# Last output rows: three column groups transposed and multiplied before the fourth; last scaling on VectorE; a borrowed score bank in unit 8

## The chip, the core and the metric

The kernel runs on one core of one Trainium2 chip. The metric is the time of one execution on the device, in microseconds, as the median of several runs. Five engines work side by side, each with an in-order queue of its own: TensorE (PE, with its weight loads PEld), VectorE (DVE), ScalarE (ACT), GpSimd (POOL) and SyncE (SP). They wait for each other through semaphores. SP and ACT also issue DMA transfers.

## What is computed

One transformer block on 2048 tokens of width 576, in float32. Six modulation rows come from a small vector c. The attention has 32 heads of 18 and goes through four segments of 512 tokens; a memory M, z is carried from segment to segment.

```python
h = _layernorm(x, axis=-1) * (1 + ca) + sa
# per segment s: masked softmax attention, mixed with the memory's answer
a_dot = softmax(q k^T * scale + mask) @ v
a_mem = (phi(q) @ M) / (phi(q) @ z + 1e-6)
o = g * a_mem + (1.0 - g) * a_dot
M, z = M + phi(k)^T v, z + sum(phi(k))
x = x + ga * (o @ wo)
h = _layernorm(x, axis=-1) * (1 + cb) + sb
x = x + gb * ((_silu(h @ w_gate) * (h @ w_up)) @ w_down)
```

Products are kept near float32 by splitting an operand into a rounded high part and a low rest (`oh` and `ol`, `woh` and `wol`) and adding the products of the parts.

## The kernel before

The work goes in three stages. The first projects q, k, v. The second, in which the change lies, goes through 32 units of four heads of one segment (8 units to a segment), from about 248 to 587 us. The third is the FFN, from 605 us to the end, in two halves of 1024 tokens.

**Order.** Everything in the second and third stage is written out by hand in program order (`tc.manual_schedule`), engine by engine; a tile pool hands out buffers in turn, and an instruction waits for the last user of the buffer that it gets. In the second stage a unit u has 11 steps. At each step one score tile of `p2_step` (line 624: a matmul into a PSUM bank, line 627: its exponential by ACT into `Pt`) and one of `p1_step` for unit u + 2 (line 189, reduced by VectorE on line 194 to row maxima `mx`) are issued, and then the events of the table `PAT`: `V` attention times values (`av`, line 644), `m`/`n` the maxima's transpose (`pmt`, `mr`), `c`/`d` the combination of a unit's result (`px`, line 665; lines 673 to 682), `R`/`S`/`T` transposes of finished output rows and their split (`pto`, lines 726, 733, 737), `Z`/`z` the same for columns 512 to 575 of four rows together (`ptr`, lines 709, 715, 716), `M`/`X` the product with `wo` and the addition of the residual (`pw`, line 753; line 758). Things due later, `stage_a` and `stage_b` among them, are put into `sched` by step.

**PSUM.** It has eight banks. In the second stage they are shared out by tags: `s2` (scores for the exponential, 2 banks), `s1` (scores for the maxima, 2), `x` (2, for `px`, `pmt`, `pto`, `ptr`, `pn`, `pt`), `w` (1) and `av` (1). In units 0 to 3 every third score tile takes a bank of tag `x` in place of one of `s2`. For the last output rows a pool of its own, `pst`, opens over the same banks, with four banks of tag `x` and two of tag `w`.

**stage_b** brings the second segment's half of the FFN's input into place in units 25 to 30: for each of six pieces four transposes of a loaded block (`trans4`, line 971, into `pt`), two scalings by columns (`scaled`, line 966, on ACT, from PSUM into `yo` and `yh`), sums and differences on GpSimd (line 1030), and a split and a store (`y_part`).

**Last output rows.** After unit 31 the fourth segment's 512 rows (`ot[3]`, 4 groups of 128) are multiplied by `wo`. The last unit's combination is the last writer of columns 504 to 575: line 681 and line 682, on VectorE here. Then:

```python
        wo_r(3, 0)
        wo_z(3)
        wo_r(3, 1)
        wo_s(3, 0)
        wo_t(3, 0)
        wo_z2(3)
        wo_s(3, 1)
        wo_t(3, 1)
```

`wo_r` makes four transposes of 128 columns, `wo_z` four of the last 64 columns, `wo_s` casts the transposed tile to `oh` on ACT, `wo_t` takes the rest `ol` on VectorE. Then four times two halves of 288 columns follow with 14 multiplies each: `oh` eight times, `ol` four times, the last 64 columns (`orr`) twice. The transposes of groups 2 and 3 stand behind the multiplies of groups 0 and 1. Weights for the FFN are prepared in between. The addition of the residual for the row group before, (2, 3), is done on VectorE (line 758) just behind line 682, and its store is issued from ACT (line 760).

Of the kernel before, what the change touches and what calls it, by code (L numbers as in the profile page):

```python
# [7 lines left out]
F32 = mybir.dt.float32  # L8
F32R = mybir.dt.float32r
BF16 = mybir.dt.bfloat16  # L10
AF = mybir.ActivationFunctionType
ALU = mybir.AluOpType
# [3 lines left out]
P = 128  # L16
# [49 lines left out]
S1B, S2B, XB, WB = 2, 2, 2, 1  # L66
# [7 lines left out]
def block(ctx: ExitStack, tc: tile.TileContext, x, wqk, wv, wo, beta, wgu, wd, c, w_mod, wm01, out):  # L74
    nc = tc.nc
# [30 lines left out]
    ident = cst.tile([P, P], F32, tag="ident", name="ident")  # L106
# [28 lines left out]
    colm = cst.tile([P, 6, 2], F32, tag="colm", name="colm")  # L135
# [11 lines left out]
    xD = [dr.tile([P, 4, D], F32, tag=f"xD{s}", name=f"xD{s}") for s in range(NSEG)]  # L147
# [11 lines left out]
    turn = [0, 0]  # L159
# [93 lines left out]
    with ExitStack() as p1:  # L253
# [6 lines left out]
        ps = pool(p1, "ps1", 2, space=PSUM)  # L260
# [73 lines left out]
        with ExitStack() as p0:  # L334
# [39 lines left out]
            for b in range(3):  # L374
                n = P if b < 2 else 64
# [233 lines left out]
    def p2_step(u, j):  # L609
        if u >= NU:  # L610
            return
        n = L - 128 * j
        per = L // n if n <= 256 else 1
        pt = pp_.tile([P, 4, n], F32, tag=f"P{j}", name="Pt", bufs=1)
        Pt[u, j] = pt
        for h in range(0, 4, per):
            turn[1] += 1
            if u < 4 and turn[1] % 3 == 0:
                bank = ps.tile([P, L], F32, tag="x", name="s2", bufs=XB)
            else:  # L620
                bank = ps.tile([P, L], F32, tag="s2", name="s2", bufs=S2B)
            for g in range(h, h + per, 2):
                w = min(per, 2)
                nc.tensor.matmul(bank[:, n * (g - h):n * (g - h + w)].rearrange("p (a b) -> p a b", a=w),  # L624
                                 lhsT=kst[u % NB][0:110, g // 2, 128 * j:128 * j + 128],
                                 rhs=qst[u % NB][0:110, g:g + w, 128 * j:L], start=True, stop=True)
            nc.scalar.activation(pt[:, h:h + per, :n], bank[:, :n * per].rearrange("p (a b) -> p a b", a=per),  # L627
                                 AF.Exp, scale=SCALE)
            if h + per < 4:
                yield  # L630
        nc.gpsimd.affine_select(out=pt[:, :, :P], in_=pt[:, :, :P], pattern=[[0, 4], [1, P]], compare_op=ALU.is_ge,
                                fill=0.0, base=0, channel_multiplier=-1)
        yield
# [50 lines left out]
    ot, vq = {}, {}  # L684
# [13 lines left out]
    def yh(k, kb):  # L698
        return yh12[:, k - 1, kb] if k else yh0[:, kb]
# [18 lines left out]
    def load_xr(s, i):  # L718
        xr = o3.tile([P, D], F32, tag="xr", name="xr") if s < 3 or i in (0, 3) else xp.tile([P, D], F32, tag="xs", name="xr")
        nc.sync.dma_start(xr, x[s][:, i, :])  # L720
        return xr

    def wo_r(s, i):
        pt = ps.tile([P, 4, P], F32, tag="x", name="pto", bufs=XB if s < 3 else 4)
        for kt in range(4):
            nc.tensor.transpose(pt[:, kt, :], ot[s][:, i, 128 * kt:128 * kt + 128], ident)
        pto[s, i] = pt
        oh = o3.tile([P, 4, P], F32R, tag="oh", name="oh")
        ol = o3.tile([P, 4, P], F32R, tag="ol", name="ol")
        oT[s, i] = (oh, ol, load_xr(s, i) if s < 3 else xr3[i])  # L730

    def wo_s(s, i):
        nc.scalar.copy(oT[s, i][0], pto[s, i])

    def wo_t(s, i):
        oh, ol, _ = oT[s, i]
# [4 lines left out]
    def wo_m(s, i, h, c, wb=WB):  # L741
        oh, ol, _ = oT[s, i]
        sl = slice(288 * h, 288 * h + 288)
        if c == 0:
            wps[0] = ps.tile([P, L], F32, tag="w", name="pw", bufs=wb)
        ops = []
        for k in range(4):
            ops += [(oh[:, k], woh[:, k, sl]), (oh[:, k], wol[:, k, sl]), (ol[:, k], woh[:, k, sl])]
        if s == 3:
            ops = [ops[n] for n in (0, 1, 3, 4, 6, 7, 9, 10, 2, 5, 8, 11)]  # L750
        ops += [(orr[s][:, i], woh[:, 4, sl]), (orr[s][:, i], wol[:, 4, sl])]
        for n in range(14 * c // WC, 14 * (c + 1) // WC):
            nc.tensor.matmul(wps[0][:, :288], lhsT=ops[n][0], rhs=ops[n][1], start=(n == 0), stop=(n == 13))  # L753

    def wo_x(s, i, h):
        xr = oT[s, i][2]
        sl = slice(288 * h, 288 * h + 288)
        nc.vector.tensor_tensor(xr[:, sl], wps[0][:, :288], xr[:, sl], op=ALU.add)
        if h == 1:
            (nc.scalar if (s, i) == (2, 3) else nc.sync).dma_start(xD[s][:, i, :], xr)  # L760

    lnv = {}

# [197 lines left out]
            for j in range(3):  # L961
                nc.sync.dma_start(dst[:, :, 32 * j:32 * j + 32], src)

    def scaled(dst, pt, kh, kb):
        n, c = P if kb < 2 else 96, 3 * kh + kb
        nc.scalar.activation(dst[:n], pt[:n], AF.Identity, scale=colm[:n, c, 0:1], bias=colm[:n, c, 1:2])

    def trans4(xb, n, pts, key):
# [28 lines left out]
    def stage_b():  # L997
        big = flat(sk2.tile([P, 5, L], F32, tag="pq", name="yq"))
        sts = [big[:, L * i:L * i + L].rearrange("p (a b) -> p a b", b=256).bitcast(F32R) for i in range(2)]
        xb = [big[:, L * i:L * i + L].rearrange("p (a b) -> p a b", b=P) for i in (2, 3)]  # L1000
        sub = flat(opl_.tile([P, 4, D], F32, tag="o1", name="yo"))
        h10 = [sub[:, 256 * i:256 * i + 256] for i in range(2)]
        t3 = [sub[:, 256 * i:256 * i + 256] for i in (2, 3)]
        sto = [sub[:, 1024 + L * i:1024 + L * i + L].rearrange("p (a b) -> p a b", b=256).bitcast(F32R) for i in range(2)]
        pts = {}

        def load(i, hv, kb):
            for kh in range(2):
                load_cols(xb[i % 2][:, 2 * kh:2 * kh + 2], 1, 2 * hv, kh, kb)

        for i in range(6):
            hv, kb = divmod(i, 3)
            u = 25 + i
            n = P if kb < 2 else 96
            c = slice(256 * hv, 256 * hv + 256)
            h00, h01, h11 = [yh(k, kb)[:n, c] for k in range(3)]
            a, b = h10[i % 2], t3[i % 2]
            at(11 * (u - 1) + 1, lambda i=i, hv=hv, kb=kb: load(i, hv, kb))
            g = step_of(u)

            def trans(i=i, n=n):
                trans4(xb[i % 2], n, pts, i)

            def sc(i=i, kb=kb, a=a, c=c):
                pt = flat(pts.pop(i))
                scaled(a, pt[:, 0:256], 0, kb)
                scaled(yh(2, kb)[:, c], pt[:, 256:512], 1, kb)

            def sub2(d, x, y_, op=ALU.subtract):
                nc.gpsimd.tensor_tensor(d, x, y_, op=op)  # L1030
            at(g, trans)
            at(g + 1, sc)
            at(g + 2, lambda b=b, h11=h11, a=a, n=n: sub2(b[:n], h11, a[:n]))
            at(g + 3, lambda h00=h00, a=a, n=n: sub2(h00, a[:n], h00))
            y_part(g + 6, 3, kb, h00, lambda i=i: sto[i % 2], hv)
            at(g + 5, lambda h01=h01, h11=h11: sub2(h01, h01, h11))
            at(g + 7, lambda h00=h00, h01=h01: sub2(h01, h01, h00, ALU.add))
            y_part(g + 4, 5, kb, b, lambda i=i: sts[i % 2], hv)
# [89 lines left out]
    def load_y(t, o):  # L1128
        nc.sync.dma_start(f32(y[:, o, 0:4]), yD[t][o][:, 0:4])
        nc.sync.dma_start(f32(y[0:96, o, 4]), yD[t][o][0:96, 4])  # L1130
# [231 lines left out]
    with tc.manual_schedule():  # L1362
# [40 lines left out]
        load_y(0, 0)  # L1403
        load_o(0, 0, 1)
        load_y(0, 1)
        xr3[3] = load_xr(3, 3)
        load_y(0, 5)
        load_y(0, 3)
        wo_r(3, 0)
        wo_z(3)  # L1410
        wo_r(3, 1)
        wo_s(3, 0)
        wo_t(3, 0)
        wo_z2(3)
        wo_s(3, 1)
# [2 lines left out]
        for i in range(4):  # L1418
            for h in range(2):
                for c in range(WC):  # L1420
                    n = 8 * i + 4 * h + c
                    wo_m(3, i, h, c, 2)
                    if c == 3:
                        wo_x(3, i, h)
                    flush()
                    if n in SS:
                        j = SS.index(n)
                        sum_o(0, j // 4, j % 4, nc.vector if j > 3 else nc.gpsimd)
                    if n == 24:
                        nc.scalar.activation(omg[:, 0:1], omg[:, 0:1], AF.Silu)  # L1430
                        store_o(0, 0)
                    if n in HH:
                        y_here(HH.index(n))
                    if n in WW:
                        j = WW.index(n)
                        if j < 2:
                            prep_r(0, 0, 0, j)
                        prep_w(0, 0, next(gw))
                if h == 1 and i < 2:
                    wo_r(3, i + 2)  # L1440
                    wo_s(3, i + 2)
                    wo_t(3, i + 2)
        flush()
# [214 lines left out]
```

## Time and profile before

| | |
|---|---|
| median of 3 runs | 1870.22 us (1869.98 to 1872.08) |
| the profiled execution | 1873.14 us, its span 1871.4 us |
| TensorE clock granted | 0.999 |
| PE busy | 1851.8 us, 99% of the span |
| DVE, ACT, POOL busy | 80%, 52%, 26% |
| share of PE in the chain that ended last | 92% |
| the second stage's end, the last output rows, the first FFN multiply | 586.4, 589.27, 605.23 us |

Times in rows are microseconds from the span's start. A row of a timeline gives the start, the duration, the engine, the line, the operation, output and inputs, shape and count, and in square brackets how long the engine was idle before it and on what. Matmuls overlap: a row's duration is longer than the time to the next one, and the end is modelled, so a short wait can lie hidden under the tail of the matmul ahead. A row of waits gives who waited for whom, the total, the number of times and the longest. `PEld` is the weight load, `ACTq` and `SPq` are issues of DMA.

### The profile page before, as it was taken

The page shows a single profiled execution, that of the slowest core. Times are in us where ns is not written, and L with a number is a line of the kernel's source. Part 1 is how long each engine was busy: PE and PEld are TensorE (multiplying, and loading weights), DVE is VectorE, ACT ScalarE, POOL GpSimd, SP SyncE. Part 2 cuts the span into 40 slices and gives each one's busy share as a digit, 9 for nine tenths or more (in the row PEclk, how much of TensorE's full clock was granted, in tenths as well). Part 3 has the DMA queues.
Part 4 walks back from the last instruction along what each step waited for, and adds up shares of the span by engine and source line. Part 5 has one row for each costly group of instructions (what it writes and reads, how often), then busy time and mean ns, then how long its engine had stood idle before and what let it go on. Part 6 is the DMA issues. An engine that isn't in the chain of part 4 may idle for free.

```text
span 1871.4 us, 30687 instructions
## 1 busy us (share of the span) xinstructions
PE 1851.8 (99%) x10933; PEld 1562.6 (83%) x10933; DVE 1496.0 (80%) x3309; ACT 967.5 (52%) x2113; POOL 489.2 (26%) x685
## 2 busy tenths in 40 slices
PE   8999999999999999999999999999999999999999
PEld 5988866777767888888888888888888888888888
DVE  7566388888886887988888889758888888888886
ACT  7444467667676645445445444434444454444441
POOL 2010045453565244554553544300000000000000
PEclk9999999999999999999999999999999999999999
DMA  8767655447556755555455444385332333333331
GB/s 302 249 221 243 219 158 151 146 144 204 162 149 233 246 188 171 164 176 195 155 167 174 147 143 161 128 286 179 119 100 89 126 104 95 108 104 126 103 101 51
DMA packets 177585, 303.43 MB, mean 162 GB/s; under 512 B 25976, under 2 KB 107512, under 8 KB 175512
## 3 DMA queue, kind: packets, MB, share of 16 engines
q1 hardware_dynamic: 150056, 247.61, 41.9%
q10 hardware_dynamic: 27376, 53.86, 8.1%
q8 instruction: 86, 1.41, 0.3%
q14 instruction: 67, 0.55, 0.1%
HBM read 187.53 MB, written 113.33 MB: 161 GB/s over the span
## 4 chain that ended last, share of the span: by engine, by line
PE 92%; DVE 3%; DMA 3%; ACT 1%; issue 1%; SPq 0%; POOL 0%; ACTq 0%; DVEq 0%
PE A L1209 23%; PE pd L1337 13%; PE C L1209 12%; PE pd L1318 10%; PE pp L100 6%; PE B L1209 6%; PE s L624 4%; PE s L189 4%; PE av L644 4%; PE pv L100 3%; PE pw L753 3%; DMA y<-yD 1%; PE pn L810 1%; PE px L665 1%; PE pm L458 1%; DVE junk L194 1%
## 5 line engine op out<-in xcount | busy, mean ns | idle before, releaser
L1209 PE MATMUL A<-y,wh 128*128 128x512 f32 x1152 | 406.9, 394 | 3.1 <-DMA y<-yD 2.0
L194 DVE CUSTOM_DVE_ANT_0 junk<-s,tri 128x256 bf16<-128x256 f32 (+3 forms) x512 | 226.4, 486 | 57.1 <-PE s L189 50.3
L1209 PEld LDWEIGHTS A<-y,wh 128*128 128x128 f32 x1152 | 217.1, 188 | 47.8 <-ACT B L1255 2.3
L1174 DVE TENSOR_TENSOR wl<-O,wh 128x256 fp32r<-128x256 f32 x504 | 247.7, 497 | 2.2 <-ACT wh L1173 1.7
L1209 PE MATMUL A<-y,wl 128*128 128x512 f32 x576 | 227.3, 395 | 0.0
L627 ACT ACTIVATE Pt<-s 128x512 f32<-128x512 f32 (+1 forms) x352 | 186.0, 559 | 73.4 <-PE s L624 67.9
L1323 DVE TENSOR_TENSOR acc<-acc,pd 128x576 f32<-128x576 f32 x216 | 162.3, 752 | 58.8 <-PE pd L1318 51.5
L1209 PE MATMUL C<-y,wh 128*128 128x512 f32 x576 | 202.9, 393 | 0.5 <-DVE cu L1232 0.5
L1173 ACT CAST wh<-O 128x256 fp32r<-128x256 f32 x504 | 197.6, 405 | 2.1 <-issue 1.1
L1347 DVE TENSOR_TENSOR acc<-acc,pd 128x576 f32<-128x576 f32 x156 | 116.9, 750 | 93.8 <-PE pd L1337 93.3
L1337 PE MATMUL pd<-dh,ah 128*128 128x288 f32 x640 | 189.2, 296 | 0.5 <-DVE x L1341 0.5
L1337 PE MATMUL pd<-dh,al 128*128 128x288 f32 x640 | 189.1, 295 | 0.0
L1337 PE MATMUL pd<-dl,ah 128*128 128x288 f32 x640 | 188.9, 295 | 0.0
L1164 POOL TENSOR_TENSOR O<-O 128x384 f32<-128x384 f32 x132 | 149.6, 1147 | 139.6 <-DVE wl L1174 29.1
L1278 ACT CAST ah<-sg 128x512 fp32r<-128x512 f32 x192 | 119.1, 620 | 77.0 <-DVE sg L1233 70.7
L624 PE MATMUL s<-qs,ks 110*128 110x512 f32 (+2 forms) x384 | 147.5, 401 | 1.4 <-ACT nm L819 0.6
L1279 DVE TENSOR_TENSOR al<-sg,ah 128x512 fp32r<-128x512 f32 x192 | 138.8, 723 | 9.7 <-ACT ah L1278 9.5
L189 PE MATMUL s<-ks,qs 108*128 108x256 f32 (+3 forms) x512 | 140.1, 325 | 0.9 <-DMA qs<-qD 0.2
L1318 PE MATMUL pd<-dh,ah 128*128 128x288 f32 x448 | 133.0, 297 | 0.0
L1318 PE MATMUL pd<-dh,al 128*128 128x288 f32 x448 | 132.5, 296 | 0.0
L1318 PE MATMUL pd<-dl,ah 128*128 128x288 f32 x448 | 132.3, 295 | 0.0
L1337 PEld LDWEIGHTS pd<-dh,ah 128*128 128x128 f32 x640 | 120.9, 189 | 6.9 <-DVE x L1341 0.8
(370 smaller groups left out, 4335.0 us busy)
## 6 DMA issues: line engine op xcount, KB each, us to landing
O<-in_wgu_dram SPq DMA_DIRECT2D x36, 768.0 KB
O<-oD SPq DMA_DIRECT2D x36, 512.0 KB
oD<-O ACTq DMA_DIRECT2D x34, 512.0 KB
ks<-kD SPq DMA_DIRECT2D x64, 216.0 KB
qs<-qD SPq DMA_DIRECT2D x64, 216.0 KB
O<-in_wgu_dram SPq DMA_DIRECT2D x36, 384.0 KB
rD<-wr ACTq DMA_DIRECT2D x36, 336.0 KB
wr<-rD SPq DMA_DIRECT2D x35, 336.0 KB
```

Of the source, the lines that this page charges most:

```text
L100: nc.tensor.matmul(ps, lhsT=a, rhs=b, start=(k == 0), stop=(k == 13))
L189: nc.tensor.matmul(bank[:, n * (h - h0):n * (h - h0) + n], lhsT=qst[b][0:108, h, 128 * i:128 * i + 128], rhs=kst[b][0:108, h // 2, 0:n], s ...
L194: nc.vector.tensor_tensor_reduce(junk[:, :n], bank[:, n * (h - h0):n * (h - h0) + n], tri[:, L - n:], 1.0, -3e38, op0=ALU.add, op1=ALU.max ...
L624: nc.tensor.matmul(bank[:, n * (g - h):n * (g - h + w)].rearrange("p (a b) -> p a b", a=w), lhsT=kst[u % NB][0:110, g // 2, 128 * j:128 * ...
L627: nc.scalar.activation(pt[:, h:h + per, :n], bank[:, :n * per].rearrange("p (a b) -> p a b", a=per), AF.Exp, scale=SCALE)
L1164: eng.tensor_tensor(o[:, d], o[:, a], o[:, b], op=op)
L1173: nc.scalar.copy(wh, o)
L1174: later.append(lambda: nc.vector.tensor_tensor(wl, o, f32(wh), op=ALU.subtract))
L1209: nc.tensor.matmul(bank, lhsT=a, rhs=b, start=(first and n == 0), stop=(n == 6), skip_group_check=not first)
L1318: nc.tensor.matmul(pd[:, i, :288], lhsT=a[:, tk], rhs=w, start=(k == 0), stop=(k == 2))
L1323: nc.vector.tensor_tensor(o, o, pd[:, :, :288], op=ALU.add)
L1337: nc.tensor.matmul(pd[:, i, :288], lhsT=a[:, tk], rhs=w, start=(k == 0), stop=(k == 5))
```

## The change

Three edits, in program order:

1. In unit 8, too, every third score tile (four of eleven) takes a bank of tag `x`.
2. The last of the six scalings of `stage_b` (i = 5) is done on VectorE by two `tensor_scalar` with a multiply and an add, in place of two ACT activations.
3. In the last output rows the first three column groups of row groups 0, 1 and 2 are transposed first (nine transposes). ACT casts three column groups of row group 0, and three multiplies of its first half are issued. The fourth column groups, `wo_z` and the cast of the fourth group follow. The store of (2, 3) is issued from ACT behind the first cast. The transposes of row group 2 no longer stand behind row group 0's multiplies.

```diff
-            if u < 4 and turn[1] % 3 == 0:
+            if (u < 4 or u == 8) and turn[1] % 3 == 0:
                 bank = ps.tile([P, L], F32, tag="x", name="s2", bufs=XB)
...
-    def wo_r(s, i):
-        pt = ps.tile([P, 4, P], F32, tag="x", name="pto", bufs=XB if s < 3 else 4)
-        for kt in range(4):
-            nc.tensor.transpose(pt[:, kt, :], ot[s][:, i, 128 * kt:128 * kt + 128], ident)
-        pto[s, i] = pt
-        oh = o3.tile([P, 4, P], F32R, tag="oh", name="oh")
-        ol = o3.tile([P, 4, P], F32R, tag="ol", name="ol")
-        oT[s, i] = (oh, ol, load_xr(s, i) if s < 3 else xr3[i])
-
-    def wo_s(s, i):
-        nc.scalar.copy(oT[s, i][0], pto[s, i])
+    def wo_r(s, i, kts=range(4)):
+        if 0 in kts:
+            pto[s, i] = ps.tile([P, 4, P], F32, tag="x", name="pto", bufs=XB if s < 3 else 4)
+        for kt in kts:
+            nc.tensor.transpose(pto[s, i][:, kt, :], ot[s][:, i, 128 * kt:128 * kt + 128], ident)
+        if 0 not in kts:
+            return
+        oT[s, i] = [None, None, load_xr(s, i) if s < 3 else xr3[i]]
+
+    def wo_s(s, i, ks=slice(0, 4)):
+        if ks.start == 0:
+            oT[s, i][0] = o3.tile([P, 4, P], F32R, tag="oh", name="oh")
+            oT[s, i][1] = o3.tile([P, 4, P], F32R, tag="ol", name="ol")
+        nc.scalar.copy(oT[s, i][0][:, ks], pto[s, i][:, ks])
...
-        if h == 1:
-            (nc.scalar if (s, i) == (2, 3) else nc.sync).dma_start(xD[s][:, i, :], xr)
+        if h == 1 and (s, i) != (2, 3):
+            nc.sync.dma_start(xD[s][:, i, :], xr)
...
-    def scaled(dst, pt, kh, kb):
+    def scaled(dst, pt, kh, kb, vec=False):
         n, c = P if kb < 2 else 96, 3 * kh + kb
+        if vec:
+            nc.vector.tensor_scalar(dst[:n], pt[:n], colm[:n, c, 0:1], colm[:n, c, 1:2], op0=ALU.mult, op1=ALU.add)
+            return
...
-                scaled(a, pt[:, 0:256], 0, kb)
-                scaled(yh(2, kb)[:, c], pt[:, 256:512], 1, kb)
+                scaled(a, pt[:, 0:256], 0, kb, i == 5)
+                scaled(yh(2, kb)[:, c], pt[:, 256:512], 1, kb, i == 5)
...
+        head = range(3)
+        for i in range(3):
+            wo_r(3, i, head)
+        wo_s(3, 0, slice(0, 3))
+        wo_m(3, 0, 0, 0, 2)
+        nc.scalar.dma_start(xD[2][:, 3, :], oT[2, 3][2])
         xr3[3] = load_xr(3, 3)
         load_y(0, 5)
         load_y(0, 3)
-        wo_r(3, 0)
+        for i in range(2):
+            wo_r(3, i, (3,))
         wo_z(3)
-        wo_r(3, 1)
-        wo_s(3, 0)
+        wo_r(3, 2, (3,))
+        wo_s(3, 0, slice(3, 4))
         wo_t(3, 0)
...
                 for c in range(WC):
                     n = 8 * i + 4 * h + c
-                    wo_m(3, i, h, c, 2)
+                    if n:
+                        wo_m(3, i, h, c, 2)
...
                 if h == 1 and i < 2:
-                    wo_r(3, i + 2)
+                    if i:
+                        wo_r(3, i + 2)
                     wo_s(3, i + 2)
                     wo_t(3, i + 2)
```

More of the change, by code (lines that the diff above doesn't have):

```diff
@@ L750, in wo_m @@
             ops = [ops[n] for n in (0, 1, 3, 4, 6, 7, 9, 10, 2, 5, 8, 11)]
-        ops += [(orr[s][:, i], woh[:, 4, sl]), (orr[s][:, i], wol[:, 4, sl])]
+        if c:
+            ops += [(orr[s][:, i], woh[:, 4, sl]), (orr[s][:, i], wol[:, 4, sl])]
         for n in range(14 * c // WC, 14 * (c + 1) // WC):
```

## Prediction

> **What bounds the kernel now.** I read the page first, then the list of who waited for whom on TensorE, then the timelines around the three places that the change touches.
>
> ```profile
> span 1871.4 us, 30687 instructions
> PE 1851.8 (99%) x10933; PEld 1562.6 (83%) x10933; DVE 1496.0 (80%) x3309; ACT 967.5 (52%) x2113; POOL 489.2 (26%) x685
> PE 92%; DVE 3%; DMA 3%; ACT 1%; issue 1%; SPq 0%; POOL 0%; ACTq 0%; DVEq 0%
> ```
>
> TensorE (PE) carries 92% of the chain that ends last and is idle for 1871.4 - 1851.8 = 19.6 us. A change that adds no multiply and takes none away can only move that idle time and the short waits hidden under matmul tails. The waits of PE over the whole span:
>
> ```profile
> PE A L1209 <- DMA y<-yD: 2.0, 1, 2.0
> PE pto L726 <- DVE o L682: 1.0, 1, 1.0
> PE px L665 <- ACT yh L966: 0.5, 1, 0.5
> ```
>
> The second is where the last output rows begin and the third is the last scaling; unit 8 shows only 0.17 (its row is below). So all that the change can win is about 1.0 + 0.5 + 0.2, plus hidden parts.
>
> **Part A, the last output rows.** PE, then VectorE (DVE), ScalarE (ACT), GpSimd (POOL), each from its timeline:
>
> ```profile
> 586.40 0.49 PE L726 MATMUL pto<-ident,o 128*128 128x128 f32 x3
> 587.92 0.33 PE L726 MATMUL pto<-ident,o 128*128 128x128 f32 x1 [1.04 <-DVE o L682]
> 588.09 0.60 PE L709 MATMUL ptr<-ident,o 128*64 128x128 f32 x4
> 588.53 0.60 PE L726 MATMUL pto<-ident,o 128*128 128x128 f32 x4
> 589.27 0.40 PE L753 MATMUL pw<-woh,oh 128*128 128x288 f32 x1
> 590.97 0.30 PE L753 MATMUL pw<-woh,or 128*128 128x288 f32 x1
> 591.23 0.29 PE L753 MATMUL pw<-woh,oh 128*128 128x288 f32 x1
> 593.10 0.60 PE L726 MATMUL pto<-ident,o 128*128 128x128 f32 x4
> 593.45 0.38 PE L753 MATMUL pw<-woh,oh 128*128 128x288 f32 x1
> 605.23 0.40 PE L1209 MATMUL A<-y,wh 128*128 128x512 f32 x1
> ...
> 586.94 0.93 DVE L682 TENSOR_TENSOR o<-o,tmp 128x288 f32<-128x288 f32 x1
> 587.79 0.45 DVE L758 TENSOR_TENSOR xr<-pw,xr 128x288 f32<-128x288 f32 x1
> 589.25 0.69 DVE L737 TENSOR_TENSOR ol<-pto,oh 128x512 fp32r<-128x512 f32 x1 [1.02 <-ACT oh L733]
> 589.98 0.68 DVE L716 TENSOR_TENSOR or<-ptr,or 64x512 fp32r<-64x512 f32 x1
> ...
> 588.27 0.33 ACTq L760 DMA_DIRECT2D xD<-xr  x1
> 588.64 0.58 ACT L733 CAST oh<-pto 128x512 fp32r<-128x512 f32 x1 [3.72 <-DMA O<-in_wgu_dram]
> 589.12 0.58 ACT L715 CAST or<-ptr 64x512 fp32r<-64x512 f32 x1
> ...
> 582.57 1.22 POOL L631 TENSOR_SCALAR_AFFINE_SELECT Pt<-Pt 128x512 f32<-128x512 f32 x2 [0.17 <-ACT Pt L627]
> 583.75 3.80 POOL L1042 TENSOR_TENSOR ys<-yh,yh 128x512 f32<-128x512 f32 x3
> ```
>
> Before: three transposes, 1.04 idle until L682 has finished the last 72 columns of o, nine more transposes (0.11 each: 588.09 to 588.53 for four), then the wait for ACT's cast, which stood behind the store's issue of 588.27 (its row names a DMA, but in the program the cast waits for PE alone). The fourth multiply of the row went at about 589.77 (589.27 plus a first one of 0.24, then 0.13 each, as 590.97 to 591.23 for two).
>
> After: nine transposes that need nothing new run from 586.40 to about 587.4, and the cast of 384 columns ends at about 587.45 (586.95 plus at most 0.58). By the intent, the three multiplies would follow at 587.5. But in the built program the new pw lies in the PSUM bank of the old pw, and the first multiply waits for VectorE's count at L758, the last reader of that bank. L758 ends at 588.24. So the wait does not go; it passes from L682 to L758, and is next over at about 588.3. Then: three multiplies to 588.8 (0.24 + 2 x 0.13), two fourth transposes, four of ptr and one more to 589.55 (7 x 0.11). The fourth multiply goes at 589.55, against 589.77: 0.2 won.
>
> That is given back within the row. The cast of the fourth group starts when its transpose is out (588.8 + 0.33) and ends by about 589.4; L737 follows to 590.1, just in time for its multiplies (589.55 + 5 x 0.13 = 590.2). But ptr now comes out at about 589.6, so L715 runs to 590.2 and L716 to 590.9, while its multiplies could go at 590.75: 0.2 lost. The row ends at about 591.25, as before (591.23). What stays is that the third group's transposes are no longer at 593.10: 593.45 - 593.10 = 0.35. The multiply behind them was also slowed by a restart, so I take **-0.3**, with ends of -1.3 (the multiplies really start at 587.5 and only L716 holds them up) and +0.3 (`or` later still, L737 missed). The store keeps its issue of 588.27: the cast now ahead of it on ACT's queue is over 0.8 earlier, and no DMA changes its place on SP's queue.
>
> L682 takes 0.93 where L758, just as wide, takes 0.45, and ends 0.32 after POOL's third ys (583.75 + 3.80 = 587.55). [...]
>
> **Part C, the last scaling.** PE, ACT, and the nearest form for VectorE reading PSUM (groups by line and shape):
>
> ```profile
> 565.56 0.60 PE L971 MATMUL pt<-ident,yq 128*96 128x128 f32 x4
> 568.80 0.66 PE L665 MATMUL px<-ident,avs 128*128 128x128 f32 x4 [0.46 <-ACT yh L966]
> ...
> 567.25 0.59 ACT L656 COPY avs<-av 128x512 f32<-128x512 f32 x1 [0.22 <-PE av L644]
> 567.73 0.56 ACT L966 ACTIVATE yo<-pt,colm 96x256 f32<-96x256 f32 x1
> 568.19 0.55 ACT L966 ACTIVATE yh<-pt,colm 96x256 f32<-96x256 f32 x1
> ...
> L447 DVE TENSOR_SCALAR pe<-ptk 128x256 f32<-128x256 f32 x3 | 1.3, 423 | 0.7 <-PE ptk L445 0.7
> 569.49 0.26 DVE L673 RECIPROCAL r<-px 128x16 f32<-128x16 f32 x1 [4.16 <-PE px L665]
> ```
>
> The two scalings leave ACT (1.0 us of its queue) and go to VectorE at 566.2, when pt is out: two of 0.42 (0.6 at most, as ACT's), over by 567.4. VectorE sat idle for 4.16 there, so nothing queues behind them. px then needs only avs (567.84) and goes at 568.34, in its turn: 0.46 won. ACT's exponentials come 0.9 earlier, which may give up to 0.15 more at the next attention multiplies. **-0.5**, ends -0.65 and 0.
>
> **Part B, unit 8.** Four of its eleven score tiles take a bank of tag x.
>
> ```profile
> 314.17 0.44 PE L624 MATMUL s<-qs,ks 110*128 110x384 f32 x1 [0.17 <-ACT Pt L627]
> 318.70 0.48 PE L624 MATMUL s<-qs,ks 110*128 110x256 f32 x2
> 321.74 0.40 PE L624 MATMUL s<-qs,ks 110*128 110x512 f32 x1
> 322.27 0.50 PE L189 MATMUL s<-ks,qs 108*128 108x512 f32 x1
> ...
> 319.24 0.69 DVE L737 TENSOR_TENSOR ol<-pto,oh 128x512 fp32r<-128x512 f32 x1
> 321.51 0.69 DVE L194 CUSTOM_DVE_ANT_0 junk<-s,tri 128x512 bf16<-128x512 f32 x1
> ```
>
> Won: waits for the exponential's evacuation, 0.17 shown at 314.17 and as much again or more hidden under tails; I take a lead of 0.5 by 318.70 (0.17 to 0.6). Lost: in the built program the unit's last score tile (the L624 of 318.70) lies in the bank that pto had, and now waits for L737, which ended at 319.93. L737 stands on VectorE behind reductions that PE feeds, so it moves by the lead: the L624 goes at about 319.98 - 0.5 = 319.5 instead of 318.2, with L189 and the attention multiplies queued behind it. That is 1.28 of new wait. A part is absorbed: before, PE waited at 322.27 for the reduction begun at 321.51, though 321.74 + 0.24 = 321.98 was free. PE alone now arrives at 321.98 + 1.28 - 0.5 = 322.76, +0.5 against 322.27, of which 0.1 of restart (a tail of 0.50 at 322.27, 0.40 otherwise) goes. **+0.4**, ends -0.6 (L737 early enough) and +1.1 (lead 0.17, nothing absorbed).
>
> **Sum.** -0.3 - 0.5 + 0.4 = -0.4 us; the ends add to -2.55 and +1.4. The profiled execution took 1873.14 us (span 1871.4 and 1.74 around it), so it would take 1872.7. The median of the three runs is 1870.22, 2.9 below the profiled one; the difference carries over to it: **1869.8 us**. From 605.23 (the first FFN multiply) PE carries the chain to the end but for stretches of VectorE work that PE releases and for DMA (fourth rival), so the lead is kept.
>
> **Rivals.** First, everything pays: the first multiplies go at 587.5, and L737 frees its bank in time: -2.5, 1867.7. For it speaks that cast and transposes are ready by then; against it, both waits in the built program. Chance 0.15.
>
> Second, slower: the bank of pto in unit 8. From the point where the lead at 318.70 falls under about 0.2, nothing offsets the 1.28, and the attention multiplies behind the L624 come 1.1 late; with A and C as forecast, +0.3: 1870.5. Against it: the wait of 322.27, which absorbs. Chance 0.07.
>
> [...] Chance 0.06.
>
> Fourth, the reload of y between the token halves, the first row of the waits (2.0 us of PE). In the chain of waits it stands as two loads:
>
> ```profile
> 1227.76 9.92 DMA y<-yD
> 1237.75 14.60 DMA y<-yD
> ```
>
> If the loads fall out of step with PE, the wait can go (with everything paid, -2.5 - 2.0 = -4.5: 1865.7), or the first load can take as long as the second, 4.7 more (-0.4 + 4.7 = +4.3: 1874.5). For it: loads of one kind differ by that much within one execution, and the kernel's own runs spread over 2.1 us, 1869.98 to 1872.08; against it: the loads are issued by what PE has read, so they should move along. Chances 0.12 and 0.08.
>
> The built program does all three things, so no case is kept for a change without effect.
>
> **Numbers.** The forecast has the remaining 0.52. A measurement of this kernel can tell about 0.2% from no change, 3.7 us. Only the fourth rival's two ends pass that: faster 0.12, within 0.80, slower 0.08. The range, 1867.0 to 1871.6, holds the forecast with the sum's ends (1867.7 to 1871.6) and the first three rivals, 0.80, with 0.7 at the low end for the runs' own spread.
>
> **What would show it.** Right: a wait of PE of about 0.9 at 587.4 on DVE's xr, none on o; px without its 0.46; a new wait of over 1 us in unit 8 on ol, and the lag at 322 under 0.5; the first FFN multiply, now at 605.23, at 604.5 to 605.2. Wrong: a wait of 1 us or none at the start of the last rows before 587.6, no wait on ol in unit 8, px still waiting (on DVE yh), or a first FFN multiply outside 602.7 to 606.6.

## The result: 6 us slower, lost 20 us behind the places that the change touches

The changed kernel takes 1876.28 us (median of 7 runs, 1874.28 to 1878.38), the kernel before 1870.20 us beside it (1869.17 to 1872.08). The ratio is 1.0031, with a 95% interval of 1.0019 to 1.0042: slower by 0.31%, where 1869.8 us with 1867.0 to 1871.6 was forecast. The profiled execution of the changed kernel took 1877.68 us, its span 1876.0 us, against 1873.14 and 1871.4 before. Two single executions behind the medians further down took far longer than all others and are left out of the ratios: 10,302.88 us, the profiled one of the kernel with the requests put back, and 3644.22 us, one of the kernel before.

The page after, span and busy times:

```profile
span 1876.0 us, 30693 instructions
PE 1852.9 (99%) x10933; PEld 1564.7 (83%) x10933; DVE 1496.0 (80%) x3311; ACT 967.4 (52%) x2112; POOL 488.5 (26%) x685
```

PE has the same number of instructions and 23.1 us of idle time in place of 19.6. Four rows of PE's waits over the whole span say where it went (the largest row, 8.0 us of waiting for a load in the first stage, was 7.8 before and is not shown):

```profile
PE C L1216 <- DVE cu L1239: 3.8, 1, 3.8
PE A L1216 <- DMA y<-yD: 2.0, 1, 2.0
PE s L624 <- DVE ol L740: 1.1, 1, 1.1
PE pw L757 <- DVE xr L762: 1.1, 2, 0.8
```

The wait on `o` (1.0) and the one on `yh` (0.5) are gone, the waits on `xr` and on `ol` that the forecast put in their places are there, and the first row is new: 3.8 us in the FFN, where before had 0.5. PE's timeline after, at the rows that answer to those of before (lines 757, 978, 1216 and 1344 were 753, 971, 1209 and 1337):

```profile
319.39 0.48 PE L624 MATMUL s<-qs,ks 110*128 110x256 f32 x2 [1.13 <-DVE ol L740]
566.04 0.60 PE L978 MATMUL pt<-ident,yq 128*96 128x128 f32 x4
568.66 0.60 PE L665 MATMUL px<-ident,avs 128*128 128x128 f32 x4
588.00 0.37 PE L757 MATMUL pw<-woh,oh 128*128 128x288 f32 x1 [0.84 <-DVE xr L762]
589.15 0.38 PE L757 MATMUL pw<-wol,oh 128*128 128x288 f32 x1
590.68 0.40 PE L757 MATMUL pw<-woh,or 128*128 128x288 f32 x1
604.62 0.40 PE L1216 MATMUL A<-y,wh 128*128 128x512 f32 x1
631.38 0.80 PE L1216 MATMUL C<-y,wh 128*128 128x512 f32 x1 [3.77 <-DVE cu L1239]
640.51 0.30 PE L1344 MATMUL pd<-dh,ah 128*128 128x288 f32 x1
```

The first FFN multiply goes at 604.62, 0.61 us *ahead* of before (605.23). The same two rows before, for the end of this stretch:

```profile
628.46 0.49 PE L1209 MATMUL C<-y,wh 128*128 128x512 f32 x1 [0.48 <-DVE cu L1232]
635.96 0.30 PE L1337 MATMUL pd<-dh,ah 128*128 128x288 f32 x1
```

The first down-projection multiply goes at 640.51 against 635.96, 4.55 us behind. From there to the span's end both need the same (1876.0 - 640.51 = 1235.49 and 1871.4 - 635.96 = 1235.44 us). In these two executions the whole loss lies between 605 and 641 us, where the change edits nothing: 35.89 us from the first FFN multiply to the first down-projection multiply, 30.73 before.

**Where it comes from.** The chain of waits after, followed back from the late matmul:

```profile
605.30 6.22 DMA xD<-xr
...
613.21 8.54 DMA oD<-O
...
621.80 5.54 DMA O<-in_wgu_dram
...
630.72 0.61 DVE cu L1239
...
631.38 3.36 PE C L1216 x7
634.73 2.71 PE A L1216 x7
```

Read it forwards: the store of the last row group, issued at 605.30, lands at 611.52; only then does SP issue the first load of down-projection weights (line 1188); the load of the next O tile and the store of O (line 1155) stand behind that on SP's queue; the store lands 8.54 us after its issue, and the second O load waits for it; VectorE waits for that load (2.83 us) with `cu` queued behind; PE waits for `cu`. SP's own timeline, before and then after:

```profile
606.35 1.99 SPq L1181 DMA_DIRECT2D dr__8745<-in_wd_dram  x2
611.23 0.33 SPq L1142 DMA_DIRECT2D O<-in_wgu_dram  x1
611.62 0.62 SPq L1148 DMA_DIRECT2D oD<-O  x1
618.36 0.34 SPq L1142 DMA_DIRECT2D O<-in_wgu_dram  x1
```

```profile
611.61 1.02 SPq L1188 DMA_DIRECT2D dr__8746<-in_wd_dram  x2
612.82 0.33 SPq L1149 DMA_DIRECT2D O<-in_wgu_dram  x1
613.21 0.62 SPq L1155 DMA_DIRECT2D oD<-O  x1
621.80 0.33 SPq L1149 DMA_DIRECT2D O<-in_wgu_dram  x1
```

and the row of SP's waits (585 to 645 us) that before does not have:

```profile
SPq L1188 <- DMA xD<-xr: 5.9, 2, 3.7
```

The order of the transfers is unchanged. The weight load is 5.3 us late because it now waits for two stores. They are those of the first and the last of the last four row groups; the `xr` of the other two lies in another pool. Counted from the first FFN multiply, the second O load is 4.05 us later than before (17.18 against 13.13): 2.20 because the store of O is issued later (8.59 against 6.39), and 1.85 because the load then has to wait longer for it (8.59 against 6.74).

**Why it waits.** The weights' tile `dr` is put into memory that the pool of the last rows (`o3`) gives up. In that pool each tag gets its place in the order in which the tags are first requested. Before, `wo_r` requested `oh`, `ol` and then the residual `xr`; in the built program `dr` covers bytes 173,728 to 181,792 of each partition, `oh` begins at 176,800 and `xr` at 184,992. So `dr` lay over `oh` and the start of `ol` and waited for their last readers, PE's multiplies. The change moved the requests for `oh` and `ol` into `wo_s`, which runs after `wo_r` has requested `xr`. Now `xr` begins at 176,800 and `oh` at 181,408, so that both buffers of `xr` lie under `dr`, and `dr` waits for the last readers of `xr`: the stores.

**The second part of the loss.** After the wait the seven C multiplies take 3.36 us and the seven A multiplies 2.71, where seven take 1.61. The windows of the changed kernel (duration, busy time of PE, PEld, DVE, ACT, POOL, then PEclk, the granted clock; DMA share; GB/s):

```profile
629.00:631.00 2.00, 0.00 (x0) 0.00 (x0) 1.97 (x4) 0.00 (x0) 0.00 (x0) 0.79 1.09 390
631.00:633.00 2.00, 1.62 (x4) 1.35 (x5) 1.97 (x5) 0.92 (x3) 0.00 (x0) 0.50 1.09 389
...
635.00:637.00 2.00, 2.00 (x6) 1.63 (x5) 1.97 (x4) 0.19 (x1) 0.00 (x0) 0.50 1.02 264
637.00:639.00 2.00, 2.00 (x10) 1.61 (x9) 1.13 (x4) 1.41 (x3) 0.00 (x0) 1.00 1.05 372
```

The granted clock fell during the wait (0.79 from 629 to 631) and stayed at 0.50 until about 637. Counted from the first FFN multiply, the waiting matmul is 3.53 us late (631.38 - 604.62 = 26.76 against 628.46 - 605.23 = 23.23), and from it to the first down-projection multiply 1.63 more go (9.13 against 7.50). Together 5.16.

### The profile page after: what moved, and what is told of

The parts are those of the page before. It is cut to its first block, busy times and chain, and to the rows that moved or that the text cites. A ratio compares the mean times of both kernels' runs of the same rounds, so it can differ in the third digit from the quotient of the medians.

```text
span 1876.0 us, 30693 instructions
## 1 busy us (share of the span) xinstructions
PE 1852.9 (99%) x10933; PEld 1564.7 (83%) x10933; DVE 1496.0 (80%) x3311; ACT 967.4 (52%) x2112; POOL 488.5 (26%) x685
## 4 chain that ended last, share of the span: by engine, by line
PE 93%; DMA 3%; DVE 2%; ACT 1%; issue 0%; POOL 0%; SPq 0%; POOLq 0%; DVEq 0%; ACTq 0%
PE A L1216 23%; PE pd L1344 13%; PE C L1216 12%; PE pd L1325 10%; PE pp L100 6%; PE B L1216 6%; PE s L624 4%; PE s L189 4%; PE av L644 4%; PE pv L100 3%; PE pw L757 3%; DMA y<-yD 1%; PE pn L814 1%; PE px L665 1%; PE pm L458 1%; DVE junk L194 1%
## 5 line engine op out<-in xcount | busy, mean ns | idle before, releaser
L1216 PEld LDWEIGHTS C<-y,wh 128*128 128x128 f32 x576 | 108.8, 189 | 24.6 <-DVE cu L1239 4.2
```

What stands on the lines that cost most here:

```text
L1216: nc.tensor.matmul(bank, lhsT=a, rhs=b, start=(first and n == 0), stop=(n == 6), skip_group_check=not first)
```

## Experiments

Beside each time stand the runs of the kernel before on the same chip and the ratio with its 95% interval. "The stretch" is the time from the first FFN multiply to the first down-projection multiply in the profile, 30.73 us before and 35.89 after.

### The order of the requests put back

```diff
-        oT[s, i] = [None, None, load_xr(s, i) if s < 3 else xr3[i]]
+        if s < 3:
+            oh = o3.tile([P, 4, P], F32R, tag="oh", name="oh")
+            ol = o3.tile([P, 4, P], F32R, tag="ol", name="ol")
+        oT[s, i] = [oh, ol, load_xr(s, i)] if s < 3 else [None, None, xr3[i]]
...
-        if ks.start == 0:
+        if s == 3 and ks.start == 0:
```

> The changed kernel, with one thing put back: for the first three blocks of rows the two tiles of the transposed rows (oh, ol) are requested ahead of the tile of the residual (xr), as in the kernel before, so that oh and ol lie again in the memory that the first load of down-projection weights takes over. Layout theory: that load is issued near 606.3 us again and not at 611.6, the wait of 3.77 us at 631.38 and the slow matmuls behind it go, and what the three edits gained by 604.6 us stays: 1870.2 - 0.6 = 1869.6 us. Rival (the loss comes from the moved store of the third block's last row, or from the new order of the transposes, and not from the memory): 1876 us as with the whole change.

Measured: 1870.49 us, before 1870.08, ratio 1.0002 (0.9993 to 1.0011). With all three edits in place the loss is gone. Its profile comes from a second run.

> The changed kernel with oh and ol requested ahead of xr, a second time, for its profile. Layout theory: the load of down-projection weights goes out within 1 us of the last x store's issue (near 606 us), the O load near 611 us, no wait above 0.6 us on PE between 605 and 640 us, and the first down-projection matmul near 635.3 us, 0.6 us ahead of the 635.96 of before. Rival: the wait of 2 us or more near 631 us is there.

Measured: 1870.15 us, before 1870.25, ratio 1.0005 (0.9995 to 1.0015). The load goes out at 605.75, PE's longest wait between 600 and 660 us is 0.5, and the first down-projection multiply goes 0.60 ahead of before:

```profile
605.75 2.43 SPq L1191 DMA_DIRECT2D dr__8746<-in_wd_dram  x2
...
604.63 0.40 PE L1219 MATMUL A<-y,wh 128*128 128x512 f32 x1
635.36 0.30 PE L1347 MATMUL pd<-dh,ah 128*128 128x288 f32 x1
```

The stretch is 30.73 us, as before. The moved store and the new order of the transposes cost nothing here.

### The order of the requests alone

```diff
+        xr = load_xr(s, i) if s < 3 else xr3[i]
         oh = o3.tile([P, 4, P], F32R, tag="oh", name="oh")
         ol = o3.tile([P, 4, P], F32R, tag="ol", name="ol")
-        oT[s, i] = (oh, ol, load_xr(s, i) if s < 3 else xr3[i])
+        oT[s, i] = (oh, ol, xr)
```

> The kernel before, with only the order of three requests for tiles changed: xr ahead of oh and ol. No instruction is added, removed or moved by it. Layout theory: the load of down-projection weights waits for the stores of the first and the last of the last four rows, as in the changed kernel, PE waits near 631 us for 3 to 4 us, and the time is 1870.2 + 5.2 = 1875.4 us (4.6 us of the two spans and the 0.6 us that the changed kernel was ahead at 604.6), from 1873.5 to 1878. Rival (moved store, new order of the transposes): 1870.2 us, no change.

Measured: 1875.21 us, before 1870.08, ratio 1.0024 (1.0016 to 1.0033). One request moved ahead of two others, with no instruction added, removed or moved, brings 5.1 us of the 6.1. In its profile SP waits for the same stores, PE waits for the same `cu`, and the clock halves behind a wait of 2.25 us:

```profile
SPq L1182 <- DMA xD<-xr: 4.4, 2, 2.2
...
608.22 0.40 PE L1210 MATMUL A<-y,wh 128*128 128x512 f32 x1
633.23 0.50 PE L1210 MATMUL C<-y,wh 128*128 128x512 f32 x1 [2.25 <-DVE cu L1233]
...
634.00:636.00 2.00, 2.00 (x6) 1.52 (x5) 2.00 (x5) 1.54 (x4) 0.00 (x0) 0.51 0.84 300
```

The wait is shorter than the 3 to 4 us that were expected, and the stretch is 33.23 us: this execution lost 2.5 us there, not 5.2. The two x stores landed sooner (the weights go out at 613.73, 5.51 us behind the first FFN multiply, where the changed kernel has 6.99), and the store of O took 7.9 us in place of 8.5. The first FFN multiply itself is 3.0 us late in this execution; that comes from a wait for a load at 301.62 us, shown in the last section, where the other profiles wait 1.3 us at most. So how long the stores take differs from run to run, and with it the loss, and this one profile does not show where all of the median's 5.1 us lie. In the next kernel's profile the stretch alone is 5.65 us longer.

### The new order of the last rows alone, as it stands and with the requests put back

> Only the new order of the last rows, exactly as the change has it (oh and ol requested in the scaling helper, so behind xr). Layout theory: this edit carries the whole loss by the requests that it moved: 1875 to 1876 us. Rival (the loss needs the scaling on VectorE or the borrowed bank as well): below 1872 us.

Measured: 1875.28 us, before 1870.25, ratio 1.0027 (1.0016 to 1.0039); the stretch is 36.38 us, against 30.73 before. This edit carries the loss alone.

> Only the new order of the last rows, with oh and ol requested ahead of xr as in the kernel before. By the difference of the traces between 566 and 605 us this order is worth 0.2 us: 1870.2 - 0.2 = 1870.0 us. If the moved store or the new order of the transposes cost anything that the traces have not shown: above 1871.5 us.

Measured: 1870.75 us, before 1870.25, ratio 1.0001 (0.9991 to 1.0010); the stretch is 30.73 us.

### The wait filled with work

```diff
+                    if t == 0 and p == 1 and k == 1:
+                        fill = ps.tile([P, 2, L], F32, tag="dn", name="pd", bufs=2)
+                        for i in range(14):
+                            nc.tensor.matmul(fill[:, 0, :], lhsT=y[:, 0, 0, 0:P], rhs=y[:, 0, 1], start=True, stop=True)
                     if k != 1 or prev is not None:
                         step(z, m)
```

> The changed kernel with 14 added matmuls (128x512, 0.23 us apart, into a bank that nothing reads) placed on PE ahead of the matmul that waited 3.77 us at 631.38. They fill about 3.3 us of that wait and take nothing from the chain that ends it (loads, VectorE). Clock theory: the loss has two parts, the wait itself and the half granted clock behind it (0.50 from 631 to 637 us, where 13 matmuls stand 0.43 us apart in place of 0.23: 2.6 us); with PE kept at work the clock stays at 1.00 and the time falls by 1.7 to 2.6 us, to 1874.2 us. Rival (the slow matmuls come from late operands or from the transfers, not from the idle time): 1876.3 us, or up to 1.5 us more in executions in which the wait is shorter than the added work.

Measured: 1875.03 us, before 1870.77, ratio 1.0021 (1.0012 to 1.0030). Against the whole change (1.0031) the intervals overlap, so the time alone doesn't decide; the trace does:

```profile
627.43 3.40 PE L1513 MATMUL pd<-y 128*128 128x512 f32 x14
631.14 0.50 PE L1216 MATMUL C<-y,wh 128*128 128x512 f32 x1 [0.30 <-DVE cu L1239]
...
632.00:636.00 4.00, 3.74 (x17) 2.74 (x16) 4.00 (x9) 2.49 (x6) 0.00 (x0) 1.00 0.95 299
...
638.65 0.30 PE L1344 MATMUL pd<-dh,ah 128*128 128x288 f32 x1
```

With PE at work the clock stays at 1.00, and from the waiting matmul to the first down-projection multiply it takes 7.51 us, as before (7.50), in place of 9.13. The transfers run on beside it (a DMA share of 0.95 here). So the slow matmuls came from the idle time and not from the transfers. The whole stretch is 34.78 us, 1.1 less than in the changed kernel, since the wait itself ended 0.5 us later in this execution. The size was less than the 2.6 us expected: at full clock 0.3 us waits on ScalarE's copies come back that the slow matmuls had hidden. 1.6 us is what the half clock costs here.

### The weight load behind the load and the store of O

```diff
-        load_d(0, 0)
         seq = [(p, z, m) for t in range(2) for p in range(NPR) for z in range(2) for m in MP]
...
                             store_o(0, 1, nc.sync)
+                            load_d(0, 0)
```

> The changed kernel, tiles as it has them, with the load of the down-projection weights put behind the load of the next O tile and the store of O on SP's queue, so that the two don't queue behind its wait for the x stores. Queue theory: the O load goes out near 611.2 us again and the store near 611.6 (1.6 us earlier than in the changed kernel), the wait on PE shrinks to 2 us or less, and the time is between 1870 and 1873.5 us. Rival (it is the traffic: 576 KB of weights that now move beside the O load and the store, so that the store lands 8.54 us after its issue): no gain, 1876 us; and worse than that if VectorE, whose queue has the scaling of these weights at 615.3 us, now waits for them.

Measured: 1871.72 us, before 1870.77, ratio 1.0005 (0.9996 to 1.0013). SP's rows, SP's waits from 611 to 621 us, and the row of VectorE that takes the weights:

```profile
609.75 0.33 SPq L1149 DMA_DIRECT2D O<-in_wgu_dram  x1
610.43 0.62 SPq L1155 DMA_DIRECT2D oD<-O  x1
611.67 1.09 SPq L1188 DMA_DIRECT2D dr__8804<-in_wd_dram  x2
...
SPq L1149 <- DMA oD<-O: 4.2, 1, 4.2
SPq L1149 <- DVE wl L1181: 3.2, 1, 3.2
...
617.70 0.76 DVE L1194 TENSOR_TENSOR dr__8804<-dr__8804,gbB 128x576 f32<-128x576 f32 x1 [2.45 <-DMA dr__8804<-in_wd_dram]
```

The tiles lie as in the change, and the weights go out no earlier (611.67), yet most of the loss is gone: the stretch is 32.53 us in place of 35.89. What hurt most was not the late weights but what queued behind them on SP. The store of O lands 6.5 us after its issue (611.67 + 1.09 + 4.2 = 616.96, against 610.43). It takes about 6.6 to 7.8 us in the eight profiles in which the weights are not late, before among them (6.7), and 7.9 to 9.0 in the four with late weights just ahead of it, the changed kernel among them (8.54). Whether the weights' traffic is what slows it was not tried apart from the order on the queue. The last 1.8 us of the stretch fit the weights' own lateness: VectorE waits 2.45 us for them, `wl` stands behind that on its queue, and the second O load waits 3.2 us for `wl`.

### The other two edits, alone or together

> The kernel before, with only the last scaling moved from ScalarE to VectorE; the order of tiles is as before. By the traces a lag of 0.47 us at 565.5 us became a lead of 0.40 us at 569.6 us over this place: 1870.2 - 0.9 = 1869.3 us if nothing behind it takes that up; 1869.9 us if the wait of the last rows for the read of the last bank does. A rival that puts the loss on VectorE's added work (POOL or VectorE late for the FFN): above 1871 us.

Measured: 1870.07 us, before 1870.08, ratio 0.9997 (0.9988 to 1.0006).

> The kernel before with only the borrowed bank in unit 8. By the changed kernel's trace a lead of up to 0.87 us by 317.7 us turned into a lag of 0.47 us at 322.7 us behind the wait for the read of the borrowed bank (1.13 us on VectorE's ol). 1870.2 + 0.5 = 1870.7 us. Rival (part of the lead and lag is scatter of the early loads): 1870.2 us, no change; it is a loss of about 1.3 us against its own start at 317 us in either case.

Measured: 1871.09 us, before 1870.77, ratio 1.0003 (0.9994 to 1.0012).

> The changed kernel without the borrowed bank in unit 8, and with oh and ol requested ahead of xr: the scaling on VectorE and the new order of the last rows stay. Layout theory: no wait near 631 us, and without the 0.47 us that unit 8 lost (322.74 against 322.27) the FFN starts 1.1 us ahead of before: 1869.1 us. If the lag of unit 8 is taken up by later waits anyway: 1869.6 us. Rival (moved store, order of the transposes): 1875.5 us.

Measured: 1869.73 us, before 1870.08, ratio 1.0001 (0.9992 to 1.0010). None of these sizes can be told from nothing by the time. The traces can tell them, because a distance between two rows of one trace repeats to about 0.1 us. From the `px` row ahead of unit 8's last part to the attention row behind it (305.29 and 322.70 before) it is 17.39 to 17.48 us in eight kernels without the borrowed bank, before among them, and 18.02 to 18.05 in five with it: unit 8 costs 0.6 us. From there to the first FFN multiply it is 282.53 before and 282.57 to 282.64 in the three other kernels that have neither of the later edits; 281.67 with the scaling alone; 282.36 with the last rows alone (twice); 281.45 to 281.55 with both. So the scaling brings 0.9 us and the last rows 0.2.

### A version with two steps of the second half swapped

PE's wait of 0.4 to 2.1 us for the reloaded y shows in most of the profiles (the "1.5 to 2.1 us in every trace" of the next text is too much: it was 0.9 in the kernel with the requests alone), and the clock sometimes halves behind it (granted clock from 1252 to 1256 us: 0.57 before, 1.00 in the kernel without the borrowed bank). For this step another stands ready one place later:

```diff
-                    z, m = ZM[PRIME[k] if prev is None else k]
+                    z, m = ZM[PRIME[k] if prev is None or t == 1 and p == 0 and k in (6, 7) else k]
```

> The scaling on VectorE and the new order of the last rows, oh and ol requested ahead of xr, no borrowed bank in unit 8, and one thing more: at the start of the second half of the tokens two steps of the FFN (7 matmuls each) change places, so that the step that waits for the last reloaded part of y (1.5 to 2.1 us at 1252 us in every trace) comes 3.2 us later. If the reload lands no later than now (1252.3 us): the wait goes, and the half clock that follows it in some executions (1252 to 1255 us in the profile of before) too: 1869.7 - 2 = 1867.7 us, down to 1866. If another load or bank is late in its place: 1869.7 us.

Measured: 1868.69 us, before 1870.77, ratio 0.9993 (0.9984 to 1.0002). PE shows no wait between 1200 and 1300 us, and this is the lowest median of all the kernels run. It is over 7 us below the changed kernel, but the interval takes in 1: against the kernel before, a gain is likely and not shown.

> The kernel before, with only the two steps at the start of the second half of the tokens in the other order. If what the version with all three things gained (1868.69 against 1870.77 us) comes from this swap: 1870.2 - 1.5 = 1868.7 us, with no wait on PE at 1252 us. If it comes from the scaling and the last rows: 1870.2 us.

Measured: 1869.49 us, before 1870.25, ratio 0.9998 (0.9989 to 1.0007). The wait on y is gone here too, but PE waits 0.9 us for another load in its place:

```profile
PE A L1209 <- DMA wr<-rD: 0.9, 1, 0.9
```

So the swap takes this wait away, and in one of its two profiles the next load is late in its place.

## Why the prediction was wrong, point by point

- **Part A, the last rows, -0.3: right.** The wait passed from `o` to `xr` as forecast (0.84 us, over at 588.00; 588.3 was said), the fourth multiply went at 589.15 (589.55 was said), with PE 0.39 earlier than before at the start of these rows (586.01 against 586.40), and the `or` multiplies went at 590.68 against 590.97. GpSimd's sums moved along with PE (583.37 against 583.75), and L682, again 0.93 us long, ended at 587.48 in place of 587.87. Measured over the part: -0.2.
- **Part C, the scaling, -0.5: right in kind, too small.** `px` goes without a wait. Measured -0.9, beyond the end of -0.65. The row shows 0.6 by 568.66: pt was 0.48 behind before at 566.04 against 565.56, and px is 0.14 ahead. The other 0.3 came just behind it: from px to the attention multiplies it was 1.23 us before (568.80 to 570.03) and is 0.97 after (568.66 to 569.63). "Up to 0.15" was given to exponentials that ScalarE starts earlier; px itself, with no wait ahead of it, also takes 0.35 us to the next row in place of 0.48 (568.66 to 569.01 against 568.80 to 569.28), which the sum left out. How the rest is shared is not shown.
- **Part B, unit 8, +0.4: right in kind, a little low.** The new wait of the last score tile on `ol` is there (1.13 us). Measured +0.6, inside its ends.
- **The sum, -0.4 by 604.6 us: right.** The three measured terms give -0.5; the first FFN multiply was forecast at 604.5 to 605.2 and came at 604.62.
- **"So the lead is kept": the step that failed.** The working ended at 605.23 and took the FFN as unchanged, because no instruction of it was moved and no DMA had changed its place on SP's queue. The order was right. But the place of a tile in memory is part of what an instruction waits for, and the diff moved two requests for tiles. SP's load of weights got a new wait on two stores (5.9 us of SP's time), the queue behind it was late, and 5 us more than offset the gain of 0.5. The part of the argument that listed what each queue waits for stopped at the last rows. The load of weights at 606.35, the next thing on SP, was never asked what it waits for.
- **The rivals.** None was this one. The first needed the multiplies at 587.5 and a free bank in unit 8, and both waits were there. The fourth had a slower end of 1874.5 with a chance of 0.08, for another load at another place (1228 us); that the time came near it is chance. Its wait of 2.0 us at the switch was indeed loose: in profiles of kernels with the same work there it is anything from none to 2.1 us. The times of the first two, 1867.7 and 1870.5, are far from the measured one.
- **The range.** It held the scatter of the known terms only. What no term covered was more than five times the largest of them.

None of the points named as showing the forecast wrong lay behind 606.6 us. The loss began where they ended.

## What to carry to other kernels

When a diff moves a request for a buffer, ask where every tile of that pool now lies and what the next pool puts on top of it: the wait appears at the first user of that memory, which can be in the next stage. Here the load into a tile that lay over the source of two stores waited 5.9 us for them to land (the later one landed 6.22 us after its issue); with the tile over a matmul's operands it went out at 606.35 without that wait. And what stands behind such a wait on a DMA queue can cost more than the transfer that waits: with the weights put behind the load and the store of O, 3.36 of the 5.16 us went (35.89 to 32.53).

## What the hardware showed that was not expected

TensorE's clock halved behind waits of about 2 us, and it did not do so each time. The windows of before behind its wait of 1.99 us at 1252, a row and window of the version without the borrowed bank with a wait of 2.08 at the same place and the full clock behind it, and the row and windows of the kernel with the requests alone behind a wait of 1.74:

```profile
1252.00:1256.00 4.00, 3.52 (x10) 2.90 (x11) 0.00 (x0) 0.24 (x1) 0.00 (x0) 0.57 1.06 298
```

```profile
1252.70 0.47 PE L1219 MATMUL A<-y,wh 128*128 128x512 f32 x1 [2.08 <-DMA y<-yD]
...
1252.00:1256.00 4.00, 3.30 (x20) 3.02 (x21) 0.00 (x0) 0.89 (x2) 0.00 (x0) 1.00 1.05 285
```

```profile
301.62 0.47 PE L624 MATMUL s<-qs,ks 110*128 110x512 f32 x1 [1.74 <-DMA qs<-mr]
...
300.00:304.00 4.00, 2.38 (x7) 1.71 (x8) 1.46 (x7) 1.91 (x4) 1.78 (x7) 0.87 0.68 190
304.00:308.00 4.00, 4.00 (x31) 2.51 (x31) 2.06 (x8) 2.04 (x6) 2.15 (x4) 0.71 0.36 118
```

At the 0.50 that was granted behind the wait of 3.77 us, a granted clock of 0.57 over 4 us is half clock for (1 - 0.57) x 4 / 0.5 = 3.4 us, and 0.87 with 0.71 over 8 us make (0.13 + 0.29) x 4 / 0.5 = 3.4 us as well; both are estimates. The changed kernel has the same behind its own wait of 1.99 us at 1257 (0.78 and 0.80 over the 8 us from 1256). After the wait of 3.77 us it lasted about twice that, from 630 to 637.

Waits of 1.74, 1.99 (twice) and 2.25 us had the half clock behind them in four places, and one of 2.08 had the full clock in another. So a wait of 2 us cost up to 1.7 us more than itself, an estimate: half of 3.4 us, where nothing hides it. In the profile of before the seven A multiplies behind the wait took 3.25 us, the next seven A multiplies 1.62. The length of the wait alone does not say whether the clock halves; what else decides it is not shown.
